# Dealing the rows of nine 64 KB stores to four DMA engines instead of sixteen

## The chip, the cores and the metric

The kernel runs on one core of one Trainium2 chip. The metric is the device time of one execution in microseconds. The time before is the median of three runs.

## The reference

The kernel computes one decode step of a block and all its gradients. The block is a layer norm, then two branches on the normed row `xn` in parallel, attention on a cache and a gated linear layer, both added to `x`. There are two batch rows of one token.

```python
xn = layernorm(x)                                   # x: 2 x 1 x 576
q  = xn @ wq                                        # 576 x 4096, 32 heads of 128
p  = softmax(q @ k.T * 128 ** -0.5)                 # 16 cached heads, 4096 positions
a  = (p @ v) @ wo                                   # wo: 4096 x 576
h  = (xn @ w_gate) * (xn @ w_up)                    # 576 x 4608 each
out = x + a + h @ w_down                            # w_down: 4608 x 576
grads = vjp(out, grad_out)  # of x, k_cache, v_cache, wq, wo, w_gate, w_up, w_down
```

The nine outputs are `out`, the gradient of `x`, the gradients of the two caches (2 x 16 x 4096 x 128 each) and those of the five weights (`out_4` to `out_8`: wq, wo, w_gate, w_up, w_down), all in bf16. The caches are 32 MiB each, so the kernel moves 92.48 MB in and as much out.

A weight gradient such as that of `w_up` is the outer product of the two rows of `xn` with the two rows of the gradient behind the product. Its 576 rows are the 576 features of `xn`: four blocks of 128 and a tail of 64.

## The kernel before

The work is written as many Python generators ("streams"): loads, transposes, scores, softmax, the outer products and the stores. A planner in the same file, the class `Order`, gives every step a cost, an engine and a priority, runs all streams against modelled clocks of the engines and of the DMA, and emits the instructions in the order that it finds. The order on each engine is thus fixed when the kernel is built. The costs, priorities and offsets are tables of numbers at the head of the file. The change touches none of them, and the copy that it adds has no step of its own in the plan.

All loads and stores but the first two small ones are issued from SyncE (SP), in one queue. A load of a cache head or a store of a cache gradient is one DMA of 1 MB, 128 rows of 8 KB. Buffers come from pools: sixteen big tiles shared by caches, transposed tiles, stores and the gated layer's weights; five weight tiles `ww`; two tail tiles `tl` of 128 x 512.

The gated layer goes in nine steps of 512 columns (`mlp`). Each step computes `D2`, the gradients behind the gate and up products, and from it the outer products. The big part of these gradients, rows 0 to 511, is stored in bunches of four steps (`grads`, `wide_outer`). The tail, rows 512 to 575, is done in each step by `tail_outer` (line 814): one `tl` tile takes the gate gradient's 64 rows on partitions 0 to 63 and the up gradient's on partitions 64 to 127. For each of four column groups `a` and both halves `w`, TensorE multiplies a stationary block of 64 columns of `xnr` (line 826), the normed rows spread over the partitions, with `D2`; an evacuation on ACT (line 470) or DVE (line 472) writes the tile. Then `put` issues two stores from SP (line 696), 64 rows of 1 KB each: first the gate half to `out_6`, then the up half to `out_7`. In HBM two neighbouring rows lie 9,216 bytes apart. The same function also stores the tail of wq's gradient, with one half alone (`nw` is 1), eight times.

`xnr` is made once, near the start, in `front`: `widen` (line 634) spreads the normed row over the partitions on TensorE and copies it out on ACT. `xi` is a small tile of two partitions which `front` uses just before that, to transpose the 64 tail features (line 628).

At the very end the kernel issues the rows of `out` and of the gradient of `x` from the tile `xy` (line 1486, two rows of 1,152 bytes each). The last instruction of SP (line 1588) waits for the outstanding stores.

Of the kernel before, what the change touches and what calls it, by code (L numbers as in the profile page):

```python
# [12 lines left out]
BF16 = mybir.dt.bfloat16  # L13
P = 128


def view(t, p0, np_, off, dims):

    (pstep, _), *_ = t.ap
    return bass.AP(t.tensor, t.offset + p0 * pstep + off, [[pstep, np_], *[list(d) for d in dims]])  # L20
# [226 lines left out]
def PE(stream, issue=0.0, quad=None, kind="f"):  # L247
    return ("op", "PE", max(CLK * stream, issue) + 0.03, quad, stream, issue, kind)


def DVE(cost):
    return ("op", "DVE", cost)


def ACT(cost):
    return ("op", "ACT", cost)
# [6 lines left out]
def EV(cols):  # L263
    return ("any", [("ACT", 0.16 + cols * 0.00083, 0.0), ("DVE", 0.145 + cols * 0.00104, cols / 1024 * BIAS)])


def ACQ(tag):
    return ("acq", tag)


def REL(tag, i):
    return ("rel", tag, i)


def WAIT(*events):
    return ("wait", events)


def SET(event):
    return ("set", event)  # L280


def SPAWN(gen, prio):
    return ("spawn", gen, prio)


def PRIO(prio):
    return ("prio", prio)


def DMA(engine, cost, nbytes, row=8192):
    packet = 0.0364 * row + 8.7
    return ("dma", engine, cost, 0.02 + nbytes / 16e3 * packet / row, packet)
# [49 lines left out]
PR = {"turn0": 1475.9, "turn1": 1614.7, "att": -4652.5, "dsc": -2890.4, "conv": 226.3, "con": -1413.1, "out1":  # L343
      3893.4, "out0": 2308.0, "front": 679.0, "back": 881.2, "W0": -1279.8, "W1": -624.6, "BD1": 2069.1, "BD0":
      -1551.4, "mlp": -735.6, "wout": -435.6, "store": -3305.7, "load": -1982.4, "wload": -3953.8, "fin": 5877.7,
      "const": 11595.3, "mload": -2275.6}
# [8 lines left out]
def kernel(  # L355
# [22 lines left out]
    nc = tc.nc  # L378
# [17 lines left out]
    FS = 512  # L396
# [7 lines left out]
    const = ctx.enter_context(tc.tile_pool(name="const", bufs=1))  # L404
# [54 lines left out]
    def events(n):  # L459
        return [Event() for _ in range(n)]  # L460
# [7 lines left out]
    def cp(e, out, in_):  # L468
        if e == "ACT":
            nc.scalar.copy(out, in_)  # L470
        else:
            nc.vector.tensor_copy(out=out, in_=in_)  # L472

    ctx.enter_context(tc.manual_schedule())
    ident = const.tile([P, P], BF16, name="ident")
# [4 lines left out]
    xnr = const.tile([P, D], BF16, name="xnr")  # L480
    dyr = const.tile([P, D], BF16, name="dyr")

    def filled(name, shape, dtype, value, eng=nc.vector):
        t = const.tile(list(shape), dtype, name=name)
        eng.memset(t[:], value)
        return t
# [10 lines left out]
    acc = filled("acc", [P, 5, 2], FP32, 0.0)  # L497
    accx = filled("accx", [P, 144], FP32, 0.0)
    xs = filled("xs", [P, 6, 32], BF16, 0.0)
    xi = filled("xi", [2, 2, P], BF16, 0.0)  # L500
    Wdy = filled("Wdy", [P, 2, 160], BF16, 0.0)

    for t in (*W_t[0], *W_t[1], *wm_t, *oT_t):
# [68 lines left out]
    def widen(src, dst):  # L572
        i = yield ACQ("o")
        o = o_t[i]
        yield PE(0.24)
        for k in range(2):
            nc.tensor.matmul(o[:, k, 0:HD2], lhsT=sel2[:].rearrange("b a m -> b (a m)"),
                             rhs=src[:, k * HD2:(k + 1) * HD2], start=True, stop=True)
        e = yield EV(D)
        cp(e, dst[:].rearrange("p (k n) -> p k n", k=2), o[:, :, 0:HD2])  # L580
        yield REL("o", i)
# [17 lines left out]
    def front():  # L599
        xb = xy[:, 0:D]  # L600
        yield DMA("ACT", 0.45, 2304, 1152)
        nc.scalar.dma_start(xb, A_x.rearrange("b s d -> (b s) d"))
        nc.scalar.dma_start(xy[:, D:2 * D], grad_out.rearrange("b s d -> (b s) d"))
        yield ("lset", Ein)
        yield ACT(1.5)
        nc.scalar.activation(warm[:], eps_t[0:1], AF.Sqrt)
        yield WAIT(Ein)
        yield DVE(1.0)
        for k in range(2):
            nc.vector.bn_stats(bst[:, k], xb[:, k * HD2:(k + 1) * HD2])  # L610
        nc.vector.bn_aggr(mv[:], bst[:].rearrange("p k s -> p (k s)"))
        yield ACT(0.3)
        nc.scalar.activation(rstd[:], mv[:, 1:2], AF.Sqrt, bias=eps_t[:], scale=1.0)
        yield DVE(0.6)
        nc.vector.reciprocal(rstd[:], rstd[:])
        nc.vector.tensor_scalar(xnb[:], xb, mv[:, 0:1], rstd[:], op0=ALU.subtract, op1=ALU.mult)
        yield ACT(1.5)
        nc.scalar.activation(warm[:], eps_t[0:1], AF.Exp)

        yield DVE(0.12)  # L620
        nc.vector.tensor_copy(view(xi[:], 0, 2, 0, [[P + 1, 2], [2, 64]]), view(xnb[:], 0, 2, 512, [[0, 2], [1, 64]]))
        i = yield ACQ("m")
        tp = m_t[i][:].bitcast(BF16)
        yield PE(0.02, 0.16)
        for c in range(4):
            nc.tensor.transpose(tp[:, 2 * c:2 * c + 2], xnb[:, c * P:(c + 1) * P], ident[0:2, 0:2])
        for h in range(2):
            nc.tensor.transpose(tp[:, 8 + 2 * h:10 + 2 * h], xi[:, h], ident[0:2, 0:2])
        yield DVE(0.16)
        nc.vector.tensor_copy(xs[:, :, 0:2], tp[:, 0:12].rearrange("p (c b) -> p c b", b=2))  # L630
        yield REL("m", i)
        yield SET(Exn)
        yield WAIT(Edy)
        yield from widen(xnb, xnr)
        yield SET(Exr)

        yield PRIO(PR["const"])
        yield WAIT(Econst)
        nr = gg[0:2, 0, 0:4]
        yield DVE(0.3)  # L640
        nc.vector.memset(gg[:, 1], 0.0)
        nc.vector.tensor_scalar(nmu[:], mv[:, 0:1], -1.0, None, op0=ALU.mult)
        nc.vector.tensor_scalar(nr[:, 0:2], identf[0:2, 0:2], nmu[:], None, op0=ALU.mult)
        nc.vector.tensor_scalar(nr[:, 2:4], identf[0:2, 0:2], rstd[:], None, op0=ALU.mult)
        i = yield ACQ("m")
        tp, bp = m_t[i], m_t[i][:, 64:68]
        yield PE(0.0, 0.3)
        for a in range(4):
            for c in range(4):
                nc.tensor.matmul(tp[32 * c:32 * c + 32, 2 * a:2 * a + 2], lhsT=xb[:, P * c + 32 * a:P * c + 32 * a + 32],  # L650
                                 rhs=ident[0:2, 0:2], start=True, stop=True)
        for a in range(4):
            nc.tensor.matmul(tp[0:16, 8 + 2 * a:10 + 2 * a], lhsT=xb[:, 512 + 16 * a:528 + 16 * a],
                             rhs=ident[0:2, 0:2], start=True, stop=True)
        nc.tensor.matmul(bp, lhsT=view(ones[:], 0, 2, 0, [[0, P]]), rhs=nr, start=True, stop=True)
        yield DVE(0.9)
        nc.vector.tensor_copy(xnT[:, 0:8], tp[:, 0:8])
        nc.vector.tensor_copy(xnT[0:16, 8:16], tp[0:16, 8:16])
        nc.vector.tensor_copy(nrT[:], bp)
        for k, op in ((0, ALU.add), (2, ALU.mult)):  # L660
            nc.vector.tensor_tensor(xnT[:], xnT[:], view(nrT[:], 0, P, k, [[0, 8], [1, 2]]), op)
        nc.vector.memset(gg[:, 0], 0.0)
        yield REL("m", i)
        yield SET(Eprep)
# [27 lines left out]
    def put(dst, src, nbytes, row, tag, slot, ready):  # L692
        yield WAIT(*ready)
        for d, x in zip(dst, src):
            yield DMA("SP", 0.36, nbytes, row)
            nc.sync.dma_start(d, x)
        yield ("lrel", tag, slot)
# [116 lines left out]
    def tail_outer(rhss, dsts, p, event, w0=0):  # L814
        i = yield ACQ("tl")
        st = tl_t[i]
        nw, done = len(rhss), events(2)
        yield SPAWN(put(dsts, [st[64 * w:64 * w + 64, 0:FS] for w in range(w0, w0 + nw)], 64 * FS * 2, 1024, "tl", i, done),
                    p + PR["store"])

        def mk(A):
            def mms(o):
                for w, rhs in enumerate(rhss, w0):
                    for aa in range(2):
                        a = 2 * A + aa
                        nc.tensor.matmul(o[64 * w:64 * w + 64, aa, 0:P], lhsT=xnr[32 * a:32 * a + 32, 512:576],
                                         rhs=rhs(a), start=True, stop=True)

            def ev(e, o):
                r = slice(64 * w0, 64 * (w0 + nw))  # L830
                cp(e, st[r, 256 * A:256 * A + 256].rearrange("p (a f) -> p a f", a=2), o[r, :, 0:P])
            return mms, (0.053, 0.104), 256, ev
        for A in range(2):
            yield SPAWN(unit(*mk(A), done[A]), p)
        yield WAIT(*done)
        yield SET(event)
# [675 lines left out]
    def final_dx():  # L1512
# [33 lines left out]
        yield REL("o", i)  # L1546

    od.spawn(front(), -1000.0)
    od.spawn(front_y(), -2e5)
    od.spawn(final_out(), PR["fin"])  # L1550
# [42 lines left out]
```

## Time and profile before

| what | value |
|---|---|
| time, median of 3 runs | 466.95 us (466.36 to 468.17) |
| profiled execution, its own time | 465.85 us |
| its span, first to last instruction | 464.1 us |
| mean granted TensorE clock | 0.696 |
| bytes read and written in HBM | 92.48 MB and 92.48 MB |
| tail stores, 64 KB each | 26, median 11.9 us from issue to landing |

The profile is of one execution on the chip. In a line of the slices each digit is the busy share of one fortieth of the span in tenths. "DMA share" is the mean busy share of the core's sixteen DMA engines, so that one engine alone is 0.0625. A row of a group of instructions gives the line, the engine, the operation, the tiles, how often it ran, and its duration in ns. The time to landing of a DMA goes from its issue to the last byte's arrival on the last of its engines.

### The profile page before, as it was taken

Reading aid. Unit: us, or ns where it says so; the run is one execution under the profiler, and the core shown is the slowest. Engines: PE = TensorE matmul, PEld = TensorE weight load, DVE = VectorE, ACT = ScalarE, POOL = GpSimd, SP = SyncE. Lnnn points to the kernel's source line nnn. Section 1 sums busy time; section 2 is a strip of 40 time slices with the busy share of each in tenths; the row PEclk is TensorE's granted clock in tenths of the full one; section 3 lists DMA queues with packets and bytes.
Section 4 is the critical chain, followed back from the end, with each engine's and each line's share of the span. In section 5 each row is a group of like instructions: output and inputs, shape, how many; then the busy total and the mean of one; then the engine's idle time right before and its main releaser. Section 6 shows DMA issues by size and latency. Waiting matters only on the chain. (4 is left out here: it accounts for less than half of the span.)

```text
span 464.1 us, 15709 instructions
## 1 busy us (share of the span) xinstructions
PE 372.6 (80%) x6750; PEld 213.9 (46%) x6750; DVE 366.2 (79%) x708; ACT 337.7 (73%) x515; POOL 143.1 (31%) x174
## 2 busy tenths in 40 slices
PE   1677779789986877887887788879888987976995
PEld 1444455546443444454555354644543442533543
DVE  8897888876779887778987688977966887877782
ACT  3278639868886787765867778858857987897973
POOL 0740043303316443460016251140344463053000
PEclk9978776965557676756775796755666676586955
DMA  8999999999999999999999999999999999999994
GB/s 312 416 409 422 410 426 395 408 414 372 355 415 422 407 422 407 411 423 425 414 405 418 419 423 420 424 414 411 400 406 395 394 422 424 424 404 349 422 384 186
DMA packets 40710, 185.97 MB, mean 401 GB/s; under 512 B 3640, under 2 KB 12352, under 8 KB 24256
## 3 DMA queue, kind: packets, MB, share of 16 engines
q1 hardware_dynamic: 40632, 184.96, 98.7%
q8 instruction: 53, 0.87, 0.7%
q14 instruction: 17, 0.14, 0.1%
q10 hardware_dynamic: 8, 0.00, 0.0%
HBM read 92.48 MB, written 92.48 MB: 399 GB/s over the span
## 5 line engine op out<-in xcount | busy, mean ns | idle before, releaser
L470 ACT CAST big<-ps_o 128x1024 bf16<-128x1024 f32 (+2 forms) x309 | 278.9, 963 | 50.6 <-PE ps_o L1290 23.8
L466 DVE STREAM_TRANSPOSE big<-big 128x1024 f32<-128x1024 f32 x146 | 176.4, 1223 | 18.3 <-DMA big<-in_A_v_cache_dram 8.4
L1256 POOL TENSOR_TENSOR BD<-vr,mask 128x2048 bf16<-128x2048 bf16 x32 | 115.2, 3603 | 121.6 <-DVE vr L472 49.1
L472 DVE CAST big<-ps_o 128x1024 bf16<-128x1024 f32 (+1 forms) x69 | 73.4, 1065 | 17.8 <-PE ps_o L764 7.7
L1268 PE MATMUL ps_m<-big,W 128*32 128x128 bf16 x2048 | 57.3, 272 | 4.3 <-issue 1.8
L1233 POOL COPY W<-rep 32x16 bf16<-32x16 bf16 x128 | 24.6, 192 | 115.2 <-DVE rep L1007 99.2
L1268 PEld LDWEIGHTS <-W 128*32 128x32 bf16 x2048 | 45.5, 121 | 23.5 <-issue 22.5
L1290 PE MATMUL ps_o<-BD,dd 32*128 32x512 bf16 x256 | 45.8, 523 | 9.2 <-ACT big L470 5.6
L1290 PE MATMUL ps_o<-BD,pp 32*128 32x512 bf16 x256 | 44.5, 465 | 9.1 <-ACT big L470 7.5
L466 DVE STREAM_TRANSPOSE big<-ww 128x1152 f32<-128x1152 f32 (+1 forms) x25 | 33.0, 1318 | 3.5 <-DMA out_dram<-big 3.4
L1442 PE MATMUL ps_m<-big,dd 128*32 128x512 bf16 x256 | 30.7, 578 | 1.6 <-DVE dd L466 0.9
L1442 PE MATMUL ps_m<-big,pp 128*32 128x512 bf16 x256 | 29.2, 545 | 3.5 <-DVE pp L466 2.8
L1290 PEld LDWEIGHTS <-pp 32*128 32x128 bf16 x256 | 10.3, 95 | 29.3 <-issue 25.0
L1290 PEld LDWEIGHTS <-dd 32*128 32x128 bf16 x256 | 10.7, 99 | 26.3 <-issue 18.7
L764 PEld LDWEIGHTS <-xnr 32*128 32x128 bf16 x368 | 13.6, 119 | 14.3 <-issue 13.3
L764 PE MATMUL ps_o<-D,xnr 32*128 32x128 bf16 x256 | 14.7, 285 | 4.9 <-ACT big L470 3.6
L727 PE MATMUL ps_o<-dyr,R 32*32 32x288 bf16 x256 | 17.8, 406 | 0.8 <-ACT big L470 0.7
L1039 POOL COPY qr<-qd 128x256 bf16<-128x256 bf16 x8 | 3.2, 395 | 45.8 <-DVE qd L472 43.1
L727 PE MATMUL ps_o<-dyr,hb 32*32 32x288 bf16 x288 | 15.4, 327 | 1.7 <-ACT big L470 1.6
L888 PE MATMUL ps_m<-big,Wdy 128*128 128x128 bf16 x162 | 16.2, 278 | 0.4 <-DVE cr L1394 0.3
L678 PE MATMUL ps_m<-big,wm 128*32 128x128 bf16 x416 | 13.7, 294 | 2.6 <-DVE cr L1394 1.2
L888 PEld LDWEIGHTS <-Wdy 128*128 128x128 bf16 x162 | 14.4, 127 | 3.0 <-issue 2.7
(206 smaller groups left out, 481.6 us busy)
## 6 DMA issues: line engine op xcount, KB each, us to landing
out_dram<-big SPq DMA_DIRECT2D x74, 1024.0 KB, 14.0
big<-in_A_k_cache_dram SPq DMA_DIRECT2D x32, 1024.0 KB, 14.9
big<-in_A_v_cache_dram SPq DMA_DIRECT2D x32, 1024.0 KB, 13.6
out_dram<-big SPq DMA_DIRECT2D x17, 576.0 KB, 11.0
ww<-in_B_w_down_dram SPq DMA_DIRECT2D x9, 576.0 KB, 13.1
ww<-in_A_wo_dram SPq DMA_DIRECT2D x8, 576.0 KB, 10.9
ww<-in_A_wq_dram SPq DMA_DIRECT2D x8, 512.0 KB, 10.7
big<-in_B_w_gate_dram SPq DMA_DIRECT2D x4, 1024.0 KB, 14.5
```

The source lines that it names most:

```text
L466: nc.vector.transpose(out, in_)
L470: nc.scalar.copy(out, in_)
L472: nc.vector.tensor_copy(out=out, in_=in_)
L678: nc.tensor.matmul(dp[32 * q:32 * q + 32, 0:P], lhsT=W, rhs=view(X, 0, P, xoff(q, s), [[FS, 4], [2, 32]]), start=(s == 0), stop=(s == S - 1))
L727: nc.tensor.matmul(o[32 * q:32 * q + 32, aa, 0:HD2], lhsT=view(t, 32 * q, 32, 2 * A + aa, [[4, 32]]), rhs=dyr[32 * q:32 * q + 32, k * HD2: ...
L764: nc.tensor.matmul(o[:, aa, j * P:(j + 1) * P], lhsT=xnr[32 * a:32 * a + 32, dc * P:(dc + 1) * P], rhs=rhs(a), start=True, stop=True)
L888: nc.tensor.matmul(dh, lhsT=Wdy[:, e, 2 * k:2 * k + P], rhs=view(X[:], 0, P, 64 * k + e, [[D, FC], [2, 32]]), start=(k == 0 and e == 0), s ...
L1233: nc.gpsimd.tensor_copy(view(W_t[t][w][:], 32 * a, 32, 6 + 8 * a, [[G * WW, 4], [WW, G], [1, 2]]), view(rep_t[grp[g]["qs"]][:], 32 * a, 32 ...
L1256: nc.gpsimd.tensor_tensor(BD_t[i][:], view(vr_t[v][:], 0, P, 0, [[0, 16], [1, Dh]]), view(mask16[:], 0, P, 0, [[1, 16], [0, Dh]]), ALU.mult)
L1268: nc.tensor.matmul(sc[32 * cq:32 * cq + 32, :], lhsT=view(W[:], 0, P, (be * G + l) * WW + 6 - 4 * c2 - 2 * l, [[1, 32]]), rhs=view(X[:], 0 ...
L1290: nc.tensor.matmul(o[:, k, :], lhsT=pr2[32 * c4:32 * c4 + 32, :], rhs=BD[32 * c4:32 * c4 + 32, 8 * l + 4 * h2:8 * l + 4 * h2 + 4, :], star ...
L1442: nc.tensor.matmul(ct[32 * j:32 * j + 32, :], lhsT=view(rT, 0, P, 4 * c + 2 * l, [[1, 32]]), rhs=kv_t[kvS[s][t][l]][:, Dh * c:Dh * (c + 4) ...
```

## The change

Only the second store of each pair, that of the up gradient's tail, is changed; there are nine of them. The destination is written as a three-dimensional pattern of 4 x 16 x 512: group `q` holds rows `q`, `q + 4`, `q + 8` and so on. The source stays a run of 64 partitions. So that the right rows lie there, the stationary block of the up half has its 64 columns permuted in the same way. This permuted block, `xnq`, is a copy made once on ACT, right behind `widen`. It lies in the first 64 columns of the tile `xi`, which grows from 2 to 128 partitions for it; the memset and the transposes keep to the first two.

```diff
-    xi = filled("xi", [2, 2, P], BF16, 0.0)
+    xi = const.tile([P, 2, P], BF16, name="xi")
+    nc.vector.memset(xi[0:2], 0.0)
+    xnq = xi[:, 0, 0:64]
...
-            nc.tensor.transpose(tp[:, 8 + 2 * h:10 + 2 * h], xi[:, h], ident[0:2, 0:2])
+            nc.tensor.transpose(tp[:, 8 + 2 * h:10 + 2 * h], xi[0:2, h], ident[0:2, 0:2])
...
         yield from widen(xnb, xnr)
+        nc.scalar.copy(xnq.rearrange("p (q r) -> p q r", q=4), xnr[:, 512:576].rearrange("p (r q) -> p q r", q=4))
         yield SET(Exr)
...
-        yield SPAWN(put(dsts, [st[64 * w:64 * w + 64, 0:FS] for w in range(w0, w0 + nw)], 64 * FS * 2, 1024, "tl", i, done),
-                    p + PR["store"])
+        src = [st[64 * w:64 * w + 64, 0:FS] for w in range(w0, w0 + nw)]
+        if nw > 1:
+            dsts = [dsts[0], dsts[1].rearrange("(r q) f -> q r f", q=4)]
+        yield SPAWN(put(dsts, src, 64 * FS * 2, 1024, "tl", i, done), p + PR["store"])
...
-                        nc.tensor.matmul(o[64 * w:64 * w + 64, aa, 0:P], lhsT=xnr[32 * a:32 * a + 32, 512:576],
+                        nc.tensor.matmul(o[64 * w:64 * w + 64, aa, 0:P],
+                                         lhsT=(xnq[32 * a:32 * a + 32, :] if nw > 1 and w else
+                                               xnr[32 * a:32 * a + 32, 512:576]),
                                          rhs=rhs(a), start=True, stop=True)
```

## The prediction

> **What bounds the kernel now.** I read the page first: busy shares, the slices, the DMA queues. Then the waits of SP's queue, then the DMA share in chosen stretches, down to the last microseconds, and last the rows that price the edits.
>
> ```profile
> PE 372.6 (80%) x6750; PEld 213.9 (46%) x6750; DVE 366.2 (79%) x708; ACT 337.7 (73%) x515; POOL 143.1 (31%) x174
> ...
> DMA  8999999999999999999999999999999999999994
> ...
> DMA packets 40710, 185.97 MB, mean 401 GB/s; under 512 B 3640, under 2 KB 12352, under 8 KB 24256
> ...
> q1 hardware_dynamic: 40632, 184.96, 98.7%
> ```
>
> No compute engine is above 80%, while the sixteen DMA engines are busy in every slice but the first and the last, and SP's queue alone fills 98.7% of their span. So the kernel moves bytes, and a store of 64 KB matters through the engine time it takes. A mean over sixteen engines hides how they differ. The stretches in which the mean falls show it (columns: stretch, length, busy time of PE, PE loads, DVE, ACT, POOL, the PE clock, the DMA share, GB/s):
>
> ```profile
> 112.00:116.00 4.00, 4.00 (x82) 2.97 (x76) 3.08 (x7) 3.98 (x5) 0.09 (x1) 0.50 0.71 282
> ...
> 116.00:127.00 11.00, 11.00 (x197) 5.25 (x193) 7.79 (x13) 9.76 (x14) 3.60 (x1) 0.50 1.01 354
> 127.00:227.00 100.00, 81.06 (x1421) 45.12 (x1421) 81.90 (x147) 72.24 (x112) 37.12 (x50) 0.68 1.02 417
> ...
> 417.00:419.00 2.00, 1.86 (x65) 1.25 (x57) 0.52 (x1) 1.65 (x3) 0.00 (x0) 0.95 0.67 249
> ...
> 448.00:449.00 1.00, 1.00 (x16) 0.44 (x15) 0.49 (x3) 0.80 (x1) 0.00 (x0) 0.50 0.70 243
> ...
> 457.00:458.00 1.00, 0.35 (x2) 0.21 (x3) 0.52 (x3) 0.29 (x1) 0.00 (x0) 0.50 0.13 41
> 458.00:460.00 2.00, 1.81 (x16) 0.88 (x13) 0.38 (x1) 0.15 (x1) 0.00 (x0) 0.50 0.80 267
> 460.40:461.00 0.60, 0.00 (x0) 0.00 (x0) 0.00 (x0) 0.00 (x0) 0.00 (x0) 0.50 0.07 31
> 461.20:462.60 1.40, 0.00 (x0) 0.00 (x0) 0.00 (x0) 0.00 (x0) 0.00 (x0) 0.50 0.07 24
> ```
>
> One engine of sixteen is a share of 0.0625. From 460.4 us on exactly one engine works (0.07, 24 to 31 GB/s), with every compute engine idle; in 457 to 458 two work (0.13) and fourteen have nothing queued. What that last engine still has to do stands in the DMA view of the end: first the issues, then 460.5 to 461.2, then 461.2 to 464.1.
>
> ```profile
> 453.81 0.36 SPq L696 DMA_DIRECT2D out_dram<-big  x1
> 454.59 0.47 SPq L696 DMA_DIRECT2D out_dram<-tl  x1
> 457.32 0.38 SPq L696 DMA_DIRECT2D out_dram<-big  x1
> 460.29 0.26 SPq L1486 DMA_DIRECT2D out_dram<-xy  x1
> ...
> out_dram<-big SPq DMA_DIRECT2D x1, 512.0 KB, 5.8
> ...
> DMA packets 9, 0.02 MB, mean 25 GB/s; under 512 B 3, under 2 KB 6, under 8 KB 9
> ...
> DMA packets 37, 0.04 MB, mean 12 GB/s; under 512 B 2, under 2 KB 37, under 8 KB 37
> ...
> SPq L1588 <- DMA out_dram<-big: 2.3, 2, 1.2
> ```
>
> The store issued last, the two rows of xy at 460.29, is through by 461.2: of the nine packets before that time, six are under 2 KB, which are its two rows, three closing packets and one row of the tail store. The other three are 4,608 B pieces of the store issued at 453.81. After 461.2 stand 37 packets: 35 pieces of 1 KB and two closing packets. That is one engine's whole share of the 512 KB store (32 pieces) behind three tail rows. It lands 5.8 us after its issue, at 463.1, and SP's final wait (L1588) is for it. So the end is set by one engine whose queue is about two microseconds longer than anybody else's, and the two engines that took xy's rows are not that one.
>
> **The change part by part.** The price of a row comes from the stretch in which one engine works alone:
>
> ```profile
> DMA packets 34, 0.03 MB, mean 24 GB/s; under 512 B 1, under 2 KB 34, under 8 KB 34
> ...
> L826 PE MATMUL ps_o<-D,xnr x72: 211/238/311, 45.7 to 438.7; 32*64 32x128 bf16 x72
> ...
> out_dram<-tl SPq DMA_DIRECT2D x26, 64.0 KB, 11.9
> ```
>
> In 461.2 to 462.6 it did 33 rows of 1 KB and a closing packet: 1.40 us / 33 = 0.0424 us a row, the closing one counted in. The tail pairs are the 72 matmuls of L826 that read D: nine units of eight, so 18 of the 26 tail stores, nine of them of the up weights' gradient. Today each gives every engine 64 / 16 = 4 rows, 4 x 0.0424 = 0.17 us. With four groups of sixteen, four engines get 16 rows, 0.68 us, and twelve get none. Per store: twelve engines lose 0.17 us of work, four gain 0.51. Over nine stores: -1.53 us on each of twelve, +4.58 us on each of four.
>
> Which of the two reaches the end depends on where the last engine is. The two engines of xy are off it. A rule bears on which these are: the Trainium skill, "DMA: Bandwidth & Descriptors", section "Why a DMA increments its semaphore by 16 and not by 1", says that a DMA runs on the largest k up to 16 that divides both sides' slowest dimension, and that with hardware descriptors it takes the lowest-numbered k engines. By it xy's two are among the four; the trace shows only that xy's rows went past the last engine, not the numbers. The same page of the Trainium skill, section "Latency and other measured facts", says that engines 7 and 15 are usually slower than the others; by it the last engine would be outside the four.
>
> Without numbers, four engines picked at random hold the last one in 4 cases of 16; if the four hold xy's two, 2 of the other 14 remain, 1 in 7. I take about 1 in 4, because the profile shows one execution and another could have another last engine.
>
> If the last engine is among the twelve, its queue shrinks by 0.17 us a store. How many stores count? In 112 to 116 the mean share fell to 0.71: DMA had run out of issued work, and what an engine saved before that hole may only lengthen it. The tail pairs lie here (SP issues, first at, last at, of five of the nine):
>
> ```profile
> L696 SPq DMA_DIRECT2D out_dram<-tl x2: 472/886/1300, 109.2 to 109.7; - x2
> ...
> L696 SPq DMA_DIRECT2D out_dram<-tl x2: 473/578/682, 218.9 to 219.5; - x2
> ...
> L696 SPq DMA_DIRECT2D out_dram<-tl x2: 466/671/876, 224.3 to 225.2; - x2
> ...
> L696 SPq DMA_DIRECT2D out_dram<-tl x2: 472/560/647, 276.6 to 277.2; - x2
> ...
> L696 SPq DMA_DIRECT2D out_dram<-tl x2: 472/499/526, 296.4 to 297.0; - x2
> ...
> 439.53 2.27 SPq L696 DMA_DIRECT2D out_dram<-tl  x2
> ```
>
> Four pairs come before 116 (the one at 109 is their last) and five after. So the gain lies between 5 x 0.17 = 0.85 and 9 x 0.17 = 1.53 us. I take 1.2, the middle, since the last engine need not have been idle in the hole (a share of 0.71 leaves eleven busy on average) but the compute behind the hole moves only in part.
>
> The four engines take on 4.58 us, of which 5 x 0.51 = 2.54 after the hole. What hides it is their idle time: mean idle after the hole is at least 2 x 0.33 + 0.30 + 0.87 in the rows of 417, 448 and 457, 1.8 us, and another 2.7 from 460.4 to 463.1. Only an engine that is already nearly last lacks it.
>
> The other edits:
>
> ```profile
> 10.11 0.64 ACT L470 CAST xnr<-ps_o 128x576 bf16<-128x576 f32 x1 [1.65 <-PE ps_o L577]
> 11.72 0.41 ACT L996 ACTIVATE qr<-qd 128x256 bf16<-128x256 bf16 x1 [0.98 <-DVE qd L993]
> ...
> L470 ACT COPY Q<-ps_m 128x128 bf16<-128x128 bf16 x6 | 1.8, 298 | 0.0
> ...
> L470 ACT COPY qd<-ps_m 128x8 bf16<-128x8 bf16 x3 | 0.5, 170 | 0.3 <-PE ps_m L1034 0.3
> ...
> SPq L696 <- ACT big L470: 94.8, 52, 5.2
> ```
>
> The new ACT copy of 64 columns lies between the copies of 8 columns (0.17 us) and 128 (0.30): 0.2 us. It runs once, at 10.75, into the 0.98 us in which ACT waits for DVE before L996; behind it on ACT is only that L996. Cover gone, it would cost 0.2 to 0.3 us once. The memset writes the same two rows, and the matmuls read another tile of the same shape: nothing. SP issues as many stores in the same order; a three-dimensional destination could take between the 0.47 us of the shortest tail issue and the 1.3 of the longest above. SP waits 94.8 us on ACT alone before L696, so this is hidden; without that cover it would cost up to 0.8 us a store, nine times. The rows of an up store now lie four pitches apart in HBM, still 1 KB each; the pieces priced above lie a whole row apart too, so I take no difference. On the twelve engines the store has no closing packet, so it no longer waits for the last engine; nobody is known to wait for it alone.
>
> Sum against the profiled execution: 465.85 us, its span of 464.1 and 1.75 around it; 465.85 - 1.2 = 464.65. The median of the three runs, 466.95, lies 1.1 above that execution; the same difference gives 465.75, that is 465.8.
>
> **The rivals.** 0.5% is 2.3 us, about what a measurement of this kernel can tell from no change.
>
> First, one of the four engines is the last, or becomes it: its queue grows by 2.54 (five stores) to 4.58 us (nine), 469.5 to 471.5, middle 470.5. It decides from the point where an engine of the four has less idle time than 0.68 us a store relative to the last one, 3.4 us over five. Against it: xy's two engines were idle at 460.3, and most engines idled at 417, 448 and 457. For it: in 457 to 458 a second engine was still working, and nothing names it. The Trainium skill speaks for this rival: "DMA: Bandwidth & Descriptors", section "Rules for kernel authors", wants a multiple of 16 as the outermost dimension, because an outer size of c confines a DMA to c engines. By that rule alone the change costs its 4.58 us; the row of 457 to 458, fourteen engines idle, speaks against applying it here.
>
> Second, the gain goes on past the queue: the hole at 112 to 116 closes too, 4 x 0.29 = 1.16 us, on top of 1.53: 2.7 us, 464.3. For it: stores free buffers for ACT. Against it: PE is busy 4.00 of 4.00 us in the hole, so compute sets its length.
>
> Third, the DMA is split by the 64 source partitions as before and only the row order changes: no difference, 467.0.
>
> **How the numbers follow.** Last engine among the twelve with 0.85 to 1.53 us won: 0.50. One of the four last: 0.27. Gain beyond the queue: 0.16. No effect: 0.07. Faster by over 0.5% is the second rival, 0.16; slower is the first, 0.27; within 0.5% the rest, 0.57. The range from 464.2 to 470.6 leaves out about half of either outer case, 0.08 and 0.1. The likeliest case alone spans 465.4 to 466.1.
>
> **What would show it.** Closing packets fall by 9 x 12 = 108, from 3640 under 512 B to 3532; unchanged, the third rival holds. The 512 KB store issued near the end lands in about 5 us instead of 5.8, and the single-engine stretch before the end is shorter by about a microsecond. If that stretch grows, and up stores land later than the gate stores beside them, the first rival holds and my choice of the last engine is wrong. If the share in 112 to 116 rises, the second does. ACT shows one instruction more.

## The result and the profile after

The changed kernel takes 465.02 us (median of 7 runs, 463.45 to 465.10), the kernel before, run beside it, 466.73 (7 runs, 466.11 to 468.17). The ratio is 0.9953, with a 95% interval of 0.9937 to 0.9969: 1.7 us faster. Measured a second time (below, "again") it was 1.3 us, ratio 0.9970 (0.9956 to 0.9985). The forecast was 465.8 and a gain of 1.2. The profiled execution took 464.77 us, 1.08 less than the one of before.

The page of the changed kernel, the lines that answer to the prediction's first fence:

```profile
PE 370.1 (80%) x6750; PEld 213.0 (46%) x6750; DVE 365.6 (79%) x708; ACT 337.6 (73%) x516; POOL 143.5 (31%) x174
...
DMA  8999999999999999999999999999999999999994
...
DMA packets 40602, 185.97 MB, mean 402 GB/s; under 512 B 3532, under 2 KB 12244, under 8 KB 24148
...
q1 hardware_dynamic: 40524, 184.96, 98.7%
```

Packets fell by 108, all of them among those under 512 B (3640 to 3532): nine stores with twelve closing packets fewer, as forecast. ACT has one instruction more. The busy shares say nothing else; the gain is not visible on the page. Three other views show where the two executions differ. First the stretches of the changed kernel, with the hole near 112 us (the fall of the DMA share that the prediction read there) and the end:

```profile
112.00:116.00 4.00, 4.00 (x78) 3.00 (x73) 3.10 (x7) 3.98 (x5) 0.00 (x0) 0.50 0.80 319
416.00:418.00 2.00, 2.00 (x59) 1.01 (x47) 0.49 (x1) 1.29 (x3) 0.00 (x0) 0.71 0.58 212
456.00:457.00 1.00, 0.19 (x1) 0.10 (x1) 0.67 (x4) 0.72 (x1) 0.00 (x0) 0.50 0.18 62
459.50:460.00 0.50, 0.00 (x0) 0.00 (x0) 0.00 (x0) 0.20 (x1) 0.00 (x0) 0.50 0.05 20
459.90:460.50 0.60, 0.00 (x0) 0.00 (x0) 0.00 (x0) 0.00 (x0) 0.00 (x0) 0.50 0.07 24
460.50:461.40 0.90, 0.00 (x0) 0.00 (x0) 0.00 (x0) 0.00 (x0) 0.00 (x0) 0.50 0.07 25
461.50:462.50 1.00, 0.00 (x0) 0.00 (x0) 0.00 (x0) 0.00 (x0) 0.00 (x0) 0.50 0.00 0
```

One engine alone (0.05 to 0.07) still ends the kernel, at the latest from 459.5 on and until 461.5: 2.0 us of it, beside 2.3 before, where it worked alone from 460.4 until about 462.7. Second, SP's issues at the end and its last wait:

```profile
453.23 0.35 SPq L699 DMA_DIRECT2D out_dram<-big  x1
454.02 0.51 SPq L699 DMA_DIRECT2D out_dram<-tl  x1
456.75 0.38 SPq L699 DMA_DIRECT2D out_dram<-big  x1
459.72 0.26 SPq L1493 DMA_DIRECT2D out_dram<-xy  x1
...
SPq L1595 <- DMA out_dram<-big: 1.7, 2, 1.2
```

The rows of `xy` are issued 0.57 us earlier than before (459.72 against 460.29), and the final wait for the big stores is 1.7 us instead of 2.3. In this execution, then, half of the gain lies behind the last computation and half ahead of it. Only the half ahead came back when the changed kernel was profiled a second time ("again"): there the last rows of `xy` are issued at 459.74, but the final wait for the big stores is 2.3 us as before, and one engine alone works until after 462:

```profile
459.50:460.00 0.50, 0.00 (x0) 0.00 (x0) 0.00 (x0) 0.21 (x1) 0.00 (x0) 0.50 0.07 28
...
461.50:462.00 0.50, 0.00 (x0) 0.00 (x0) 0.00 (x0) 0.00 (x0) 0.00 (x0) 0.50 0.07 25
```

Third, the chain of waits (start, length, what), its last loads of the second cache and the copy that makes `xy`; of the kernel before:

```profile
340.85 13.18 DMA big<-in_A_v_cache_dram
...
406.13 13.87 DMA big<-in_A_v_cache_dram
...
459.85 0.41 ACT xy L1482
```

and of the changed one:

```profile
339.95 12.86 DMA big<-in_A_v_cache_dram
...
404.87 14.14 DMA big<-in_A_v_cache_dram
...
459.28 0.42 ACT xy L1489
```

The first of these loads lands at 340.85 + 13.18 = 354.03 before and at 352.81 after: 1.22 us earlier. The second lands at 420.00 and 419.01, and `xy` is copied 0.57 us earlier. From the first landing to the end of the span it is 464.1 - 354.03 = 110.07 us in the one and 462.9 - 352.81 = 110.09 in the other. A lead of the size of the whole difference was thus there 110 us before the end; behind it the lead shrank to 0.57 us, and the shorter last wait made up for that. In "again" the first load lands at 353.35, 0.68 us earlier than before.

A load of 1 MB counts as landed when the last of its engines is done, and the chain waits for it. The trace also keeps when each engine reports its part of a transfer done (one increment of the transfer's semaphore from each), and these times show the last engine falling behind. In the kernel before, the last of the sixteen reports of one transfer comes 0.52 us after the second-last at 110.06 us, 1.95 at the landing of 354.03, 2.75 at that of 420.00 and 4.33 at 457.72; they don't name the engine. That an engine that lags costs time at such landings, and not only behind the last store, fits this; how much of the gain comes by this way was not measured by itself.

### The profile page after: what moved, and what is told of

It is laid out like the page before. It is cut to its first block, busy times and chain, and to the rows that moved or that the text cites. A ratio compares the mean times of both kernels' runs of the same rounds, so it can differ in the third digit from the quotient of the medians.

```text
span 462.9 us, 15711 instructions
## 1 busy us (share of the span) xinstructions
PE 370.1 (80%) x6750; PEld 213.0 (46%) x6750; DVE 365.6 (79%) x708; ACT 337.6 (73%) x516; POOL 143.5 (31%) x174
## 2 busy tenths in 40 slices
DMA packets 40602, 185.97 MB, mean 402 GB/s; under 512 B 3532, under 2 KB 12244, under 8 KB 24148
## 3 DMA queue, kind: packets, MB, share of 16 engines
q1 hardware_dynamic: 40524, 184.96, 98.7%
## 4 chain that ended last, share of the span: by engine, by line
DMA 40%; PE 28%; DVE 14%; ACT 11%; issue 5%; POOL 1%; SPq 0%; ACTq 0%; DVEq 0%; POOLq 0%
DMA out_dram<-big 24%; DMA big<-in_A_v_cache_dram 16%; ACT big L470 9%; DVE big L466 8%; PE ps_o L1297 5%; PE ps_m L1275 4%; PE ps_o L730 3%; PE ps_m L1449 3%; PE ps_m L681 2%; PE ps_m L1030 2%; DVE big L472 2%; PE ps_o L767 1%; PE ps_m L895 1%; PE ps_m L1360 1%; POOL BD L1263 1%
## 5 line engine op out<-in xcount | busy, mean ns | idle before, releaser
L1275 PE MATMUL ps_m<-big,W 128*32 128x128 bf16 x2048 | 56.1, 268 | 3.7 <-issue 1.7
L1275 PEld LDWEIGHTS <-W 128*32 128x32 bf16 x2048 | 44.4, 119 | 22.7 <-issue 21.6
L1297 PE MATMUL ps_o<-BD,pp 32*128 32x512 bf16 x256 | 45.8, 489 | 8.5 <-ACT big L470 6.8
L1449 PE MATMUL ps_m<-big,dd 128*32 128x512 bf16 x256 | 29.3, 554 | 1.2 <-DVE oT L1469 0.6
```

The lines of the kernel that those rows point to most:

```text
L1275: nc.tensor.matmul(sc[32 * cq:32 * cq + 32, :], lhsT=view(W[:], 0, P, (be * G + l) * WW + 6 - 4 * c2 - 2 * l, [[1, 32]]), rhs=view(X[:], 0 ...
L1297: nc.tensor.matmul(o[:, k, :], lhsT=pr2[32 * c4:32 * c4 + 32, :], rhs=BD[32 * c4:32 * c4 + 32, 8 * l + 4 * h2:8 * l + 4 * h2 + 4, :], star ...
L1449: nc.tensor.matmul(ct[32 * j:32 * j + 32, :], lhsT=view(rT, 0, P, 4 * c + 2 * l, [[1, 32]]), rhs=kv_t[kvS[s][t][l]][:, Dh * c:Dh * (c + 4) ...
```

## The experiments

**Theory** (the queue of the last engine): a tail store on sixteen engines costs each 0.17 us, and the kernel goes at the pace of one engine that lags; where the dealt store spares it, 0.17 us a store is won. **Rivals**: the copy, the new row order or the pattern does it; the four engines' load matters too; only some of the nine stores count; the gain is something beyond the queue. The kernels were measured in three groups, and all differences below are against the kernel before, measured beside its group on the same chip (466.40 us in the first group, 466.46 in the second, 466.63 in the third).

**The number of groups.** Three kernels deal the same nine stores in another number of groups; copy, permuted block and three-dimensional pattern stay. For sixteen groups:

```diff
-            dsts = [dsts[0], dsts[1].rearrange("(r q) f -> q r f", q=4)]
+            dsts = [dsts[0], dsts[1].rearrange("(r q) f -> q r f", q=16)]
...
-        nc.scalar.copy(xnq.rearrange("p (q r) -> p q r", q=4), xnr[:, 512:576].rearrange("p (r q) -> p q r", q=4))
+        nc.scalar.copy(xnq.rearrange("p (q r) -> p q r", q=16), xnr[:, 512:576].rearrange("p (r q) -> p q r", q=16))
```

and with 8 and 2 in the same places. "deal16", sixteen groups:

> The rows are dealt sixteen by four: the same copy on ACT, the same permuted block and the same kind of three-dimensional destination as in the change, but sixteen engines with four rows each, as before it. Theory of the queue (a store costs what it adds to the queue of the engine that ends last): no gain, 466.7 us, with 3640 packets under 512 B. Rival of the pattern (copy, row order or pattern bring the gain): 465.0 us. Rival of the early landing (the changed store lands early and so frees its tile and its place among SP's unlanded stores): no gain either, 466.7, since it still waits for the last engine.

466.71 us against 466.40, ratio 1.0008 (0.9996 to 1.0020). The gain is gone, so the copy, the order of the rows and the pattern don't make it. "deal8":

> Dealt eight by eight: eight engines get 8 rows instead of 4 (+0.17 us a store, +1.53 over nine), eight get none (-1.53). Theory of the queue: 465.0 us if the last engine is among the eight that are spared, 468.2 if it is among the eight that are loaded. Early landing: 465.0 if the landing time of these stores falls as in the change.

468.23 us, ratio 1.0040 (1.0024 to 1.0055): 1.8 us slower. Nine stores with 8 rows instead of 4 on an engine are 9 x 4 x 0.0424 = 1.53 us on each of eight. Of this kernel, the line of the packets on the page, two kinds of stretches (the hole and the end) and the chain of waits:

```profile
DMA packets 40638, 185.97 MB, mean 399 GB/s; under 512 B 3568, under 2 KB 12280, under 8 KB 24184
```

```profile
112.00:116.00 4.00, 4.00 (x67) 2.92 (x64) 3.37 (x6) 3.74 (x4) 0.00 (x0) 0.50 0.93 366
462.60:465.00 2.40, 0.00 (x0) 0.00 (x0) 0.00 (x0) 0.00 (x0) 0.00 (x0) 0.50 0.07 25
465.00:466.00 1.00, 0.00 (x0) 0.00 (x0) 0.00 (x0) 0.00 (x0) 0.00 (x0) 0.50 0.02 6
```

```profile
342.99 13.43 DMA big<-in_A_v_cache_dram
...
462.06 0.41 ACT xy L1489
```

72 packets fewer than before are 9 x 8: each store uses eight engines. The load that landed at 354.03 lands at 356.42, and one engine alone works from 462.6 until after 465, for longer than before. So the engine that lags is one of these eight, and, since four groups gain, not one of the four. This takes it that the same engine lags in every kernel, which no trace shows by name. "deal2":

> Dealt two by thirty-two: two engines get 32 rows, 28 x 0.0424 = 1.19 us more a store and 10.7 over nine (5.9 after the hole at 112 to 116), fourteen get 1.53 less. Theory of the queue: about 465.0 as long as the idle time of the two covers it, and up to 467 if they come level with the last engine. Early landing: 465.0. The rule that a DMA should use all sixteen engines: 466.7 + 10.7 = 477.4.

465.65 us, ratio 0.9988 (0.9976 to 0.9999): about half of the gain. Its 40584 packets, from the page

```profile
DMA packets 40584, 185.97 MB, mean 400 GB/s; under 512 B 3514, under 2 KB 12226, under 8 KB 24130
```

are 126 fewer than before, 9 x 14: two engines. Each of the two took on 28 x 0.0424 x 9 = 10.7 us, and nothing near that came out at the end. Fourteen engines were spared the same 1.53 us as in the change; no run shows what ate the other half.

**More stores.** "both4" deals the gate stores too, all eighteen of the pairs:

```diff
-            dsts = [dsts[0], dsts[1].rearrange("(r q) f -> q r f", q=4)]
+            dsts = [d.rearrange("(r q) f -> q r f", q=4) for d in dsts]
```

> Both stores of each pair, gate and up, are dealt four by sixteen: eighteen stores, -3.06 us on twelve engines, +9.2 on four (5.1 after the hole). Theory of the queue: a further gain of about as much as the first, 463.3 to 464.2, if the four have the idle time; 466 to 468 if one of them becomes the last. Early landing: about 463.3. If the gain is spent with the first nine: 465.0.

465.88 us against 466.40, ratio 0.9994 (0.9980 to 1.0008). The matmuls of both halves take the permuted block for it. Twice the stores give less than the nine, so saving bytes for the lagging engine alone is not the whole account. The trace fits four engines whose work tells from some point on: at the landing that was at 354.03 us, here at 354.52, the last two engines report 0.30 us apart, against 1.95 before and 3.29 in deal16, so a second one is nearly as late as the last. These are single executions, and they don't show which engines those are.

**Which of the stores.** The next kernels choose by a counter of the pairs and of the single stores of wq's tail, `n`; the flag of a half says whether it is dealt, and its matmuls take the permuted block if it is (one line of `deal` for each kernel, written together here):

```diff
+        n, pairs_n[nw > 1] = pairs_n[nw > 1], pairs_n[nw > 1] + 1
+        deal = [False] if nw == 1 else [False, n < 4]                  # early4
+        deal = [False] if nw == 1 else [False, n >= 4]                 # late5
+        deal = [n >= 4] if nw == 1 else [n >= 6, n >= 6]               # late10
+        deal = [n >= 4] if nw == 1 else [False, True]                  # up9s4
+        deal = [n >= 4] if nw == 1 else [False, n >= 4]                # late9
+        deal = [n >= 4] if nw == 1 else [n >= 4, n >= 4]               # late14
+        dsts = [d.rearrange("(r q) f -> q r f", q=4) if x else d for d, x in zip(dsts, deal)]
```

The second group, "early4" and "late5" first:

> Only the first four up stores, all before the stretch in which the DMA share falls (112 to 116 us), are dealt four by sixteen; the five later ones run on sixteen engines as before. Theory (the engine that ends last is outside the four, and what it saves before that stretch is partly lost in it): between no change and -4 x 0.17 = -0.7 us, so 466.4 to 465.7 against 466.4 for the kernel before. Rival (one of the four is the last engine in the early part, and what it takes on there is passed on to the end): +0.5 us a store, up to +2 us, 468.4. Rival (all of the change's gain comes from the early stores, through the compute behind the stretch): about -1.7 us, 464.7.

> Only the last five up stores, all after the stretch at 112 to 116 us, are dealt; the first four run on sixteen engines. Theory: the last engine saves 5 x 0.17 = 0.85 us, so 465.5 against 466.4. If the saves before the stretch count as much, this is five ninths of the change's 1.7, about 465.4, which can't be told from the former; then early4 must show four ninths of it, 465.6. Rival (the early dealt stores cost and the late ones win all of it): 464.7 or less. Rival (the gain is from the early ones): 466.4.

early4: 466.59 against 466.46, ratio 1.0001 (0.9989 to 1.0014), nothing. late5: 465.87, ratio 0.9989 (0.9979 to 1.0000), 0.6 us. The early stores alone win nothing, the late ones two thirds of 0.85. Together they are less than the change had shown, so the third group has the change once more. "late10" and "noup", the latter, whose nine stores are left out so that these rows of the output are never written, with

```diff
+        if nw > 1:
+            dsts = [dsts[0], None]
...
+            if d is not None:
+                nc.sync.dma_start(d, x)
```

> Other stores than the change's are dealt: all ten tail stores from the seventh pair on (gate and up of the last three pairs, and the four single tail stores of wq), none before. Theory: the last engine of that part is outside the four, so it saves 10 x 0.17 = 1.7 us, and the four have the idle time of the stretches near the end: 464.7 against 466.4, as good as the change or better. Rival (ten stores of +0.51 us in one part make one of the four the last): they take on 5.1 us, and if its lead over the last is under 6.8 us the result is above that: 465 to 469.

> The nine up tail stores are left out (those rows of the gradient are not written); everything else keeps its order. Every one of the sixteen engines is spared 9 x 0.17 = 1.53 us. Theory (the change takes these stores off the engine that ends last, and that is all): about the change's own gain, 466.4 - 1.5 to -1.8 = 464.6 to 464.9. Rival (the four engines' added work costs something even in the change): clearly below the change, by a microsecond or more, 463.5 or less.

late10: 465.09, ratio 0.9973 (0.9960 to 0.9985), 1.4 us. noup: 464.74, ratio 0.9969 (0.9955 to 0.9983), 1.7 us. Leaving the nine stores out altogether, with 1.53 us less on every engine, gains 1.7; dealing them gained 1.7 and, again, 1.3. By the medians the dealt stores thus come out nearly free: a cost of a microsecond from the four engines' work isn't seen, though the intervals, each over 1 us wide, don't exclude one.

The expectations have one more rival, that a changed store frees something by landing early. The rows of waits before the change give it little to free: the only wait that ends with a tail store's landing is 0.2 us of SP's last one, before the change and after it.

The third group had the change again and three selections:

> The changed kernel itself, beside a kernel before on the same chip as the next three. Four early stores alone won nothing (ratio 1.0001), five late ones 0.6 us, together less than the 1.7 us measured for all nine. If the nine together win more than their two parts, because saves add up only once the early part is lighter, this shows -1.7 us again (ratio 0.996). If the parts simply add up and the first measurement was at the upper end of its interval, -0.5 to -1.2 us (0.9975 to 0.999).

> The change's nine up stores and the last four single tail stores (of wq), which all lie in the second half, are dealt: thirteen. Theory (each dealt store takes 0.17 us off the engine that ends last, if it lies late): four more than the change, -4 x 0.17 = -0.7 us against the kernel 'again' in the same call, about 464.3, the fastest version. Rival (the four engines are full): +0.5 us a store for those four, up to 2 us above 'again'.

> The last five up stores and the last four single tail stores: nine dealt stores as in the change, but all of them after the stretch at 112 to 116 us. Theory (only the late ones count): 9 x 0.17 = -1.5 us against the kernel before, ratio 0.9967, and not slower than the change. Rival (a save counts the same wherever it lies): equal to the change.

> All fourteen tail stores of the second half (gate and up of the last five pairs, four singles) are dealt. Theory: -14 x 0.17 = -2.4 us, ratio 0.995, as long as the four engines stay ahead: they take on 14 x 0.51 = 7.1 us there, and the last engine's lead over the second was 4 us and more at the end of the earlier runs. Rival (dealt gate and up stores back to back make the four the last, as with all eighteen): no better than the change, 465 to 466.5.

"again" lies between what its expectation named: 1.3 us is more than the two parts together (-0.59 and +0.13), but within the noise of the three. All kernels with four groups in one table; "early" stores are issued before the stretch of 112 to 116 us, apart from single ones, of which only the last four are ever dealt:

| kernel | dealt, early + late | 0.17 us x all | difference of the medians | ratio and interval |
|---|---|---|---|---|
| the change | 4 + 5 | -1.53 | -1.71 | 0.9953 (0.9937 to 0.9969) |
| again | 4 + 5 | -1.53 | -1.32 | 0.9970 (0.9956 to 0.9985) |
| early4 | 4 + 0 | -0.68 | +0.13 | 1.0001 (0.9989 to 1.0014) |
| late5 | 0 + 5 | -0.85 | -0.59 | 0.9989 (0.9979 to 1.0000) |
| late9 | 0 + 9 | -1.53 | -1.40 | 0.9969 (0.9956 to 0.9982) |
| late10 | 0 + 10 | -1.70 | -1.37 | 0.9973 (0.9960 to 0.9985) |
| late14 | 0 + 14 | -2.38 | -2.19 | 0.9959 (0.9944 to 0.9973) |
| up9s4 | 4 + 9 | -2.21 | -2.61 | 0.9944 (0.9925 to 0.9963) |
| both4 | 8 + 10 | -3.06 | -0.52 | 0.9994 (0.9980 to 1.0008) |

For the late stores the gain grows with their number, 0.6, 1.4, 1.4 and 2.2 us for 5, 9, 10 and 14: 0.12 to 0.16 us a store, beside the 0.17 computed. That is the theory, for the late stores. The rival of late14 and up9s4, that the four engines are full, falls: in late14 each took on 14 x 0.51 = 7.1 us. It may hold for both4, where eight early stores are dealt: without them (late14 has the same ten late ones and four singles) there is a gain of 2.2. up9s4 is the fastest version, 464.02 us (462.48 to 465.14) against 466.63; its interval and that of the change overlap.

The chains at the same places, of early4:

```profile
341.79 13.37 DMA big<-in_A_v_cache_dram
...
461.53 0.41 ACT xy L1492
```

of late9:

```profile
340.12 13.14 DMA big<-in_A_v_cache_dram
...
459.27 0.41 ACT xy L1492
```

of up9s4:

```profile
338.42 12.93 DMA big<-in_A_v_cache_dram
...
456.98 0.41 ACT xy L1492
```

and of noup:

```profile
339.88 12.79 DMA big<-in_A_v_cache_dram
...
457.62 0.41 ACT xy L1490
```

The load lands at 355.16, 353.26, 351.35 and 352.67 us, against 354.03 before. Their spans are 466.0, 462.7, 460.6 and 462.7, so from the landing to the end they need 110.84, 109.44, 109.25 and 110.03. In these four, half or more of what an execution wins or loses against before is there at this landing. It isn't so in every kernel:

```profile
341.14 12.52 DMA big<-in_A_v_cache_dram
...
341.55 12.97 DMA big<-in_A_v_cache_dram
```

In late10 (the first line) the load lands at 353.66, 0.37 us earlier, and its span of 463.1 is 1.0 shorter; in both4 (the second) it lands 0.49 us later, and its span of 463.2 is 0.9 shorter. late10 deals only from 277 us on, and five of its ten stores come behind this landing. These are single executions, and early4's happened to be the longest of its twelve runs (467.96), up9s4's the shortest of its six (462.48); their sizes are read from the medians, and the marks only say where the difference arises.

## Why the prediction was right, point by point

**One engine sets the pace; the price of a row.** Right. At 0.0424 us a row the nine stores are 1.53 us on each engine; leaving them out won 1.72, eight groups cost 1.83 where 1.53 was computed, and late stores win 0.12 to 0.16 us each.

**Whether the last engine is among the four.** The prediction put 1 in 4 on it and could not decide it from the trace. It isn't: the change wins where the rival had 469.5 to 471.5. That the sign came out right is therefore in part luck: it was a bet at three to one on an engine that nothing in the trace had named. What the prediction held for this rival, a second engine still at work in 457 to 458, was a misreading. The DMA view of 456.2 to 458.2 in the kernel before has

```profile
q1 hardware_dynamic: 89, 0.13, 18.6%
q8 instruction: 1, 0.02, 3.5%
```

and 3.5% of sixteen engines over 2 us is 1.1 us of one engine, a single transfer of instructions. By the trace's packets it runs from 457.1 on, and of the stores and loads on SP's queue one engine alone is at work in 457 to 458. The rival's mechanism is real, and deal8 shows it: with eight groups the lagging engine is hit, and the kernel loses. The Trainium skill, "DMA: Bandwidth & Descriptors", section "Why a DMA increments its semaphore by 16 and not by 1", gives a DMA of k groups the k lowest-numbered engines; by that rule the lagging one is among the fifth to the eighth. The runs agree in that eight include it and four and two don't; the trace names no engine. The same page of the Trainium skill, "Latency and other measured facts", calls engines 7 and 15 usually slower, which would fit engine 7, but it ties this to DMAs issued from GpSimd, and the page of this kernel has 98.7% on SP's hardware queue. The rule of the Trainium skill, on the same page in "Rules for kernel authors", as the prediction used it, would make four groups cost 4.58 us here; the measurement decides against it for these stores.

**The size, 1.2 us between 0.85 and 1.53.** 1.71 in the first measurement, 1.32 in the second: the term was a little low for the one and right for the other. It was the middle of two bounds, and no run supports the half weight of the early stores that this amounts to, so the closeness is in part luck too. The prediction also held 0.5%, 2.3 us, to be about the least that a measurement can tell; the interval here is 1.5 us wide in all, so that 1.7 us could be told from nothing. Of the 0.78 us between 465.8 and 465.02, 0.22 is the base (a median of 466.95 from three runs became 466.73 with seven), 0.56 the gain.

**Early stores saved into a hole.** Half settled. early4 won nothing, below the 0.7 of a full count, as the lower bound had it. But nine stores with four early ones win as much as late9 (-1.32 and -1.40), and up9s4 at least as much; the intervals overlap, so whether an early save counts once late ones are made stays open. For the mechanism, the hole taking up what an engine saved ahead of it, the trace of before speaks: at 116.70 us the last of the sixteen engines reports 4.22 us after the first, and at 124.50, behind the hole, 0.99. Why both4's eight early stores cost so much isn't shown.

**Where the gain shows.** Here the step failed. The prediction looked for it behind the last store: about a microsecond less with one engine at work, and the 512 KB store landing in about 5 us instead of 5.8. In the first trace that stretch shrank by at most 0.3 us and the store took 5.2 us (from 456.75 to its last report at 461.94). In "again" neither sign is there: one engine worked alone from 459.5 at the latest until after 462, 2.5 us or more, and the store took 5.8 us. What both traces have is a lead at the landing of a load 110 us before the end, 1.22 and 0.68 us, and at the last computation, 0.57 and 0.55. The one engine that lags was the right cause; that its saving reaches the end through the loads that release the computation is what the traces suggest.

**The hole at 112 to 116 as a sign of the second rival.** A bad sign. Its share rose from 0.71 to 0.80, yet the gain stayed under that rival's 2.7 us. In deal16, which gains nothing, and in deal8, which loses, it rose more: 0.93 stands in the fence of deal8 above, and of deal16 there is

```profile
112.00:116.00 4.00, 4.00 (x71) 2.87 (x67) 3.45 (x6) 3.83 (x6) 0.00 (x0) 0.50 0.87 342
```

The share of a stretch of 4 us differs that much from one execution to the next, and the prediction read it from one.

**The costs put at nothing.** Right. The changed kernel's ACT at the start:

```profile
10.07 0.64 ACT L470 CAST xnr<-ps_o 128x576 bf16<-128x576 f32 x1 [1.65 <-PE ps_o L579]
10.74 0.25 ACT L637 COPY xi<-xnr 128x64 bf16<-128x64 bf16 x1
11.68 0.41 ACT L1003 ACTIVATE qr<-qd 128x256 bf16<-128x256 bf16 x1 [0.69 <-DVE qd L1000]
```

The copy took 0.25 us (0.2 forecast) and ended 0.69 us before ACT's next instruction could start. The group of SP's tail issues in the changed kernel (shortest, median and longest in ns, first and last start) is

```profile
L699 SPq DMA_DIRECT2D out_dram<-tl x26: 472/545/2400, 46.5 to 454.0; - x26
```

Nine of these 26 are three-dimensional now; the shortest issue before was 0.47 too, and the median of 0.545 us lies at the lower end of the 0.47 to 1.3 that the prediction allowed.

**What hides the four engines' work.** Right in sign, too small in size: the idle time counted from the rows of before was 1.8 + 2.7 = 4.5 us after the hole. late14 hid 7.1 us there, deal2 10.7 over the whole kernel.

## What to carry to other kernels

Where all DMA engines look busy, see whether one engine is still at work when the others have stopped: then it may be that engine's share and not the sum of the bytes that costs, and small transfers can be laid on the others. Deal a transfer in two other numbers of groups, one that keeps the lagging engine out and one that takes it in, before believing either; four groups won 1.3 to 1.7 us here, eight lost 1.8. Look for the gain at the landings that the chain waits for, not only at the end, and profile the changed kernel twice before reading a few tenths of a microsecond off one trace.

## What the runs showed of the hardware

The sixteen engines are not alike in what they can spare. In the kernel before, the last of them was done 0.52 us after the second-last at 110 us and 4.33 at 458. An engine outside the first two and four groups, but inside the eight, held the kernel back (0.75 us won with two and 1.3 to 1.7 with four, 1.8 lost with eight), while two engines took 10.7 us more work without a loss. By the medians, nine stores of 64 rows of 1 KB on four engines cost the kernel at most 0.4 us (1.32 us won by dealing them, 1.72 by leaving them out), and on sixteen 0.12 to 0.19 us each; eighteen of them, eight early, did not stay that cheap (0.52 us won in place of 3.06).
